# Tap weights broadcast over 128 rows of a cleared tile, six constant matmuls ahead of it, and a new order of all engines in a gated long convolution with a SwiGLU block

## The chip, the cores and the metric

The kernel runs on one core of one Trainium2 chip. The metric is the device time of one execution in microseconds (us); for several runs of one kernel the median is given. Beside the timed runs there is one profiled execution, whose span is the time from its first instruction to its last.

## The reference

Sequence length S = 2048, width D = 640, F = 1728, one batch, bfloat16. The input A_q is also the residual stream.

```python
x = A_q
h  = x + A(layernorm(x), A_k, A_v, A_shift_k, A_ssm_k, A_ssm_D)
h2 = h + B(layernorm(h), B_w_gate, B_w_up, B_w_down)

def A(q, k, v, shift_k, ssm_k, ssm_D):
    k_shift[s, d] = sum over t in 0..3 of k[s - 3 + t, d] * shift_k[d, 3 - t]   # causal, four taps
    kv = k_shift * v
    y  = causal convolution of kv with ssm_k along s (length 2048, by FFT), to bfloat16
    return q * (y + kv * ssm_D)

def B(x, w_gate, w_up, w_down):
    return (silu(x @ w_gate) * (x @ w_up)) @ w_down
```

The layer norms have no weights; eps is 1e-5.

## The kernel before

**Tiling.** The sequence is cut into four blocks of 512 tokens, the digit i in the names below. Tokens of a block lie on 128 partitions with four tokens to a partition (j = 0 to 3), so a block of q, k, v or of the output is a tile of 128 x 4 x 640. The long convolution is done per block in a transform domain, by matmuls with cosine and sine tables: forward transforms of the signal and of the filter, products of signal block j with filter block i - j that are summed for output block i, and an inverse transform.

**Steps and their names.** One function call builds a list of some 800 small tasks with names; each is one instruction, or for PE a short run of matmuls.

- "ident", "wrow", "k00", "k02", "kc0", "v0", "x0" and so on are loads (`load`, L446 to L449, the DMA is issued at L447). "k00" and "k02" bring token columns j = 0, 1 and j = 2, 3 of block 0 of k into k0n, "wrow" the four tap weights of each channel into two rows of the tile wrow. `tload` (L449, L450) is a load that transposes. "wrow", "drow" are issued on ACT's queue, the others on SP's.
- "zmem" (L497, POOL) fills a spare stretch of gu with ones. `filler` (L499 to L502) issues matmuls of 512 columns on it whose result nobody reads; PLAN's "fills" says ahead of which task and how many.
- "wb0", "wb4" (L510): the tap weights are spread over all partitions by matmuls of `halfrow` (two rows of ones, each for half of the partitions) with the two rows of wrow, 256 columns each, four matmuls and one. "diag0", "diag4" (L516, DVE) multiply the result with an identity, which gives the diagonal matrices of the taps.
- "k0tC.J" (L528): PE transposes block 0 of k, 20 matmuls against the identity in idall ("ident"), each for one token column J, five channel chunks C. "k0e0", "k0e2", "k0e4" copy the three results from PSUM to kT0 (L455 on ACT, L457 on DVE).
- "tpI.C" (L731): the taps as matmuls with the diagonals, in runs of 14 or 28 matmuls. "kvI.C" (L749 for block 0, L742 after) multiplies with v on DVE; for blocks 1 to 3 "keI.C" (L455) first copies PSUM into XT, which occupies the same memory as XH, the transform of the signal block two before.
- "ktM.P", "kteM.P" (L547, L455 or L457): the same transposing for filter block M. "kfM.", "xfI." are the forward transforms on PE (filter L581; signal L599 for block 0, L619 for the others), with "e" (L455, L458) for their copies from PSUM; "kb", "xb" are their additions on DVE.
- "pJI" (L777): the products on DVE, with letters a to d for their steps and "e" for the sum into the block's accumulator Y, on DVE or as an accumulating DMA. Such a DMA is `addto` (L567, L568): issued on POOL's queue, it adds one SBUF tile to another. "p02.e" adds the tile tt to Y, and p12.0a writes tt next.
- "ybI", "ivI.J" (L919, L924): the inverse transform. "ivI.Je, g, m, s, v, r, n": scaling on ACT (L934), gate by q on DVE (L941), mean and square sum on ACT (L840, L842), 1/sqrt on DVE and POOL (L835, L837), normalising on DVE (L981). "laI" are the same steps of the first layer norm.
- "htI.J" (L883): an SP-issued transposing DMA that writes the normalised 128 tokens into hnT. "fgI.HG", "fuI.HG" (L1029): gate and up matmuls of half H (256 tokens; half 0 needs htI.0 and htI.1, half 1 needs htI.2 and htI.3), group G, 20 matmuls or fewer. "sg", "su", "sv" (L1037, L1042, L1046, L1048) are their evacuations on ACT, "mu" (L1050) the product on DVE, "gd" a small copy.
- "dnI.J" (L1115, L992): the down projection, 28 matmuls. "rsI.J" writes it plus the mean to RB (L1131 on ACT, L1132 on DVE), "raI.J" is an accumulating DMA that adds RB to the residual in xh, and "outI.J" (L1144, SP) stores it. RB is one buffer. For block 3 the sum is done on DVE (L1136, L998). "xI" (L479) loads q of block I into the same xh that block I - 2 used.

**The order.** PLAN (L256 to L305) lists for each engine (pe, act, dve, pool, sp) the task numbers in the order in which the engine runs them, and for every PSUM tile which of four units of two banks it takes ("units"). An engine never runs a later task first. `add` (L92) finds what each task depends on from the memory that it reads and writes; `arrange` (L134) applies the plan, and makes the first writer of a PSUM tile wait for the readers of the tile that had the unit before; `emit` (L180) puts out the waits. A wait blocks all that stands behind it on that engine or queue.

```python
ident, id64, halfrow = idall[:, 0:P], idall[:, P:P + 64], idall[0:2, P + 64:P + 64 + P]   # L421
load("wrow", wrow[0:2], A_shift_k.rearrange("(c r x) k -> r c x k", r=2, x=64), 20000, "act")   # L469
last = e.matmul(pt.f(b // 2, 256, o=256 * (b % 2)), halfrow, wrow[0:2, c0 + b].rearrange("p x u -> p u x"), start=True, stop=True)   # L510
```

Of the kernel before, what the change touches and what calls it, by code (L numbers as in the profile page):

```python
# [12 lines left out]
P = 128  # L13
# [37 lines left out]
class _Graph:  # L51
# [128 lines left out]
    def emit(self, block):  # L180
# [74 lines left out]

PLAN = {  # L256
# [9 lines left out]
    "act":  # L266
# [10 lines left out]
    "dve":  # L277
# [10 lines left out]
    "pool":  # L288
        "19 17 15 16 125 165 174 158 192 183 223 225 224 342 396 362 281 371 285 401 380 289 406 389 343 293 420 415 527 466 "
        "470 561 474 552 478 579 570 684 586 591 529 705 710 698 637 732 723 641 645 750 649 741 "  # L290
        "",
    "sp":
        "0 2 3 8 4 6 10 7 230 9 11 13 14 235 296 226 12 229 297 227 481 231 167 176 228 234 295 233 194 185 482 232 364 282 373 "
        "290 391 294 286 382 480 653 652 471 563 554 467 475 479 581 572 651 734 725 638 752 646 743 642 650 798 807 801 804 "
        "810 "
        "",
    "units":
        "0131203132312001201201213230032110213023012230313133033220021021122013200230230222110332013110130232003210332301202110"
        "01310112312301210312031012210230131023033303012010313012013"
        "",  # L300
    "fills": {
        "wb0": ["zmem", 3],
        "k0t4.0": ["zmem", 1],
    },
}  # L305

# [1 line left out]
def bass_sequential_preLN__ssm_conv_h3__swiglu_ffn__prompt_kernel(  # L308
# [70 lines left out]
    with ExitStack() as es:  # L379
# [4 lines left out]
        def sb(name, off, shape, dty=bf):  # L384
            size = int(np.prod(shape)) * (4 if dty == f32 else 2)
            top[0] = max(top[0], off + size)
            return nc.alloc_sbuf_tensor_at(name, [P] + list(shape), dty, offset=A0 + off, align_bytes=32)
# [30 lines left out]
        kvo = sb("kvo", 179616, [4, D])  # L418
        diag = sb("diag", 184736, [NC5, 4, 64])
        idall = sb("idall", 187296, [P + 64 + P])  # L420
        ident, id64, halfrow = idall[:, 0:P], idall[:, P:P + 64], idall[0:2, P + 64:P + 64 + P]  # L421
        OS = sb("OS", 189856, [2, 2, D])
        RB = sb("RB", 187936, [D])
        bns = sb("bns", 187936 + 1280, [4, 2, 6], f32)
# [5 lines left out]
        o = 210336  # L430
# [9 lines left out]
        wrow = sb("wrow", 99840, [NC5, 64, 4])  # L440
# [3 lines left out]
        g = _Graph(nc, es)  # L444

        def load(name, dst, src, kb, engs="sp", **kw):  # L446
            return g.add(name, engs, lambda e, n: e.dma_start(dst, src), ("ld", kb), w=[dst], dma=True, **kw)  # L447
# [18 lines left out]
            load("kc%d" % m, kc[m][:], A_ssm_k[:, N * m:N * (m + 1)].rearrange("(c p) s -> p c s", p=P), 655360)  # L466

        load("ident", idall[:], id_d.ap(), 81920)
        load("wrow", wrow[0:2], A_shift_k.rearrange("(c r x) k -> r c x k", r=2, x=64), 20000, "act")  # L469
        for j in (0, 2):  # L470
            load("k0%d" % j, k0n[:, j:j + 2, :], tokens(K2, 0)[:, j:j + 2, :], 327680)
# [33 lines left out]
        for c0, nc_ in ((0, 4), (4, 1)):  # L505
            pt = g.tile()

            def mm(e, n, pt=pt, c0=c0, nc_=nc_):
                for b in range(nc_):
                    last = e.matmul(pt.f(b // 2, 256, o=256 * (b % 2)), halfrow, wrow[0:2, c0 + b].rearrange("p x u -> p u x"), start=True, stop=True)  # L510
                return last

            g.add("wb%d" % c0, "pe", mm, ("mm", 256, nc_), r=[halfrow, wrow[0:2]], pw=[pt])
            d = diag[:, c0:c0 + nc_].rearrange("p c u x -> p (c u) x")
            ib = id64.unsqueeze(1).to_broadcast([P, 4 * nc_, 64])
            g.add("diag%d" % c0, "dve", lambda e, n, pt=pt, d=d, ib=ib, nc_=nc_: e.tensor_tensor(  # L516
                out=d, in0=ib, in1=pt.f(0, 256 * nc_).rearrange("p (a x) -> p a x", x=64), op=ALU.mult),
                  ("ps", 256 * nc_), r=[id64], w=[d], pr=[pt])
# [52 lines left out]
        def halves(name, src, ev, od, scale, rot):  # L571
            for f in range(2):
                for par in (1, 0):
                    for cs in range(2):
                        pt = g.tile()
                        js = (par, par + 2)

                        def mm(e, n, pt=pt, f=f, cs=cs, js=js):
                            for j in js:
                                for c in range(2):  # L580
                                    last = e.matmul(pt.f(c, W), tab[:, f, cs, j], src[:, j, c * W:(c + 1) * W],  # L581
                                                    start=(j == js[0]), stop=(j == js[1]))
                            return last

                        g.add("%s.%d%d%d" % (name, f, par, cs), "pe", mm, ("mm", W, 4), r=[tab[:, f, cs]] + [src[:, j, :] for j in js], pw=[pt])
                        pl, sg = turn(cs, rot)
                        d = (od if par else ev)[:, f, pl, :]
                        evac("%se.%d%d%d" % (name, f, par, cs), (d, d.rearrange("p (b x) -> p b x", b=2)), lambda pt=pt: pt.f2(W), D, pt, sg * scale)
# [637 lines left out]
```

## Time and profile before

| what | value |
|---|---|
| timed runs | 260.73, 259.1, 261.67 us; median 260.73 |
| the profiled execution | 259.3 us, span 257.3 us |
| PE, DVE, ACT, POOL busy | 249.3, 200.0, 184.5, 58.5 us |
| first transpose (L528) | 4.66 us after the start of the span |
| first matmul of the signal's transform (L599) | 12.24 us |
| accumulating DMAs of 640 KB, issue to landing | C<-US 5.9 (median of 6), C<-K3r 7.9, Y<-US 6.5, Y<-tt 8.4 us |
| accumulating DMAs of 160 KB (xh<-RB) | 3.0 us, median of 12 |

Engines: PE does matmuls and PEld its weight loads, which overlap; DVE, ACT and POOL are the vector, scalar and general engines; SP issues DMAs. A line of the timeline has start, duration, engine, line of the kernel, operation, output<-inputs, count, and in brackets the idle time before it with what ended it. A busy PE is a modelled span, and single matmuls overlap, so counts times mean exceed the busy time. The chain that ended last is followed back from the last instruction to what released each step. The names there are those of the tiles, not of the tasks.

### The profile page before, as it was taken

How to read it: one execution, taken by the hardware profiler on the slowest of the kernel's cores; microseconds unless marked ns; L12 is line 12 of the kernel's file. 1: busy time of each engine (PE TensorE's matmuls, PEld its weight loads, DVE VectorE, ACT ScalarE, POOL GpSimd, SP SyncE). 2: the span in 40 equal slices, each digit the busy share in tenths (PEclk: the TensorE clock that was granted, in tenths of full speed). 3: DMA queues.
4: the chain of work that ended last, by engine and by line, in shares of the span. 5: the costliest groups of instructions: out<-in, count | busy, mean ns of one | idle time of the engine just before them, and what ended most of it. 6: DMA issues, size and time to landing. Idle time of an engine off the chain costs nothing.

```text
span 257.3 us, 5303 instructions
## 1 busy us (share of the span) xinstructions
PE 249.3 (97%) x2253; PEld 195.1 (76%) x2253; DVE 200.0 (78%) x256; ACT 184.5 (72%) x302; POOL 58.5 (23%) x56
## 2 busy tenths in 40 slices
PE   7999997999999999979999999999999999999995
PEld 4878773587888766868888866788886678888763
DVE  3689999999999998999999988999958524211242
ACT  2489999999996894577899789749981854516410
POOL 1001003082312052860030813333230314000000
PEclk9999999999999999999999999999999999999999
DMA  6998946788994058786946035497870152700011
GB/s 220 335 328 210 402 155 133 221 205 190 329 190 87 0 82 124 128 164 153 273 87 124 3 51 117 118 221 133 148 135 3 25 104 33 149 0 3 0 42 60
DMA packets 37620, 35.29 MB, mean 137 GB/s; under 512 B 21203, under 2 KB 32478, under 8 KB 37598
## 3 DMA queue, kind: packets, MB, share of 16 engines
q1 hardware_dynamic: 31792, 23.82, 33.2%
q0 software_dynamic: 5792, 11.14, 25.1%
q8 instruction: 17, 0.28, 0.5%
q14 instruction: 5, 0.04, 0.1%
q10 hardware_dynamic: 14, 0.01, 0.0%
HBM read 16.55 MB, written 2.62 MB: 75 GB/s over the span
## 4 chain that ended last, share of the span: by engine, by line
PE 62%; DVE 20%; ACT 11%; DMA 5%; issue 1%; SPq 0%; DVEq 0%
PE ps L1029 32%; PE ps L1115 16%; DVE tt L777 6%; PE ps L599 3%; DMA Y<-tt 3%; DVE Y L777 3%; PE ps L731 2%; ACT KO L455 2%; PE ps L919 2%; ACT C L455 2%; PE ps L581 2%; DVE C L777 2%; PE ps L992 2%; PE ps L619 2%; DMA k0n<-in_A_k_dram 1%; DVE gu L1050 1%
## 5 line engine op out<-in xcount | busy, mean ns | idle before, releaser
L1115 PE MATMUL ps<-Wd,gu 128*128 128x320 bf16 (+1 forms) x420 | 58.7, 300 | 0.0
L1115 PEld LDWEIGHTS ps<-Wd,gu 128*128 128x128 bf16 (+1 forms) x420 | 38.7, 97 | 18.4 <-issue 3.6
L777 DVE TENSOR_TENSOR tt<-XH,C 128x2560 bf16<-128x2560 bf16 (+1 forms) x31 | 47.8, 1571 | 1.5 <-DMA Y<-tt 0.9
L1050 DVE TENSOR_TENSOR gu<-gu,ub 128x1024 bf16<-128x1024 bf16 (+1 forms) x32 | 19.8, 620 | 26.2 <-ACT gu L1037 13.7
L1037 ACT ACTIVATE gu<-ps 128x1024 bf16<-128x1024 f32 (+1 forms) x32 | 29.4, 923 | 12.1 <-PE ps L1029 12.0
L1029 PE MATMUL ps<-hnT,GB 128*128 128x256 bf16 x280 | 34.0, 273 | 0.9 <-ACT XT L455 0.9
L1042 ACT ACTIVATE ub<-ps 128x1024 bf16<-128x1024 f32 x24 | 24.6, 1024 | 13.3 <-PE ps L1029 11.5
L1029 PE MATMUL ps<-hnT,UB 128*128 128x256 bf16 x280 | 33.8, 273 | 0.0
L1029 PEld LDWEIGHTS ps<-hnT,GB 128*128 128x128 bf16 x280 | 27.3, 98 | 4.3 <-ACT XT L455 1.0
L1029 PEld LDWEIGHTS ps<-hnT,UB 128*128 128x128 bf16 x280 | 27.3, 98 | 3.4 <-ACT KO L455 0.2
L1029 PE MATMUL ps<-hnT,GA 128*128 128x256 bf16 x240 | 28.8, 273 | 0.0
L1029 PE MATMUL ps<-hnT,UA 128*128 128x256 bf16 x240 | 28.5, 273 | 0.1
L837 POOL TENSOR_TENSOR mv<-mv,half 128x1 f32<-128x1 f32 x16 | 21.3, 1335 | 24.7 <-DVE mv L835 24.7
L1029 PEld LDWEIGHTS ps<-hnT,UA 128*128 128x128 bf16 x240 | 23.4, 98 | 3.4 <-ACT C L455 0.5
L1029 PEld LDWEIGHTS ps<-hnT,GA 128*128 128x128 bf16 x240 | 23.4, 98 | 3.2 <-DVE XH L458 0.3
L840 ACT ACTIVATE qo<-xh 128x640 bf16<-128x640 bf16 x28 | 21.0, 749 | 5.7 <-DMA xh<-in_A_q_dram 3.2
L581 PE MATMUL ps<-KT,tab 128*128 128x320 bf16 x128 | 19.6, 300 | 1.6 <-ACT K3r L455 0.7
L934 ACT ACTIVATE qo<-ps,one,st 128x640 bf16<-128x640 f32 x16 | 13.7, 886 | 9.8 <-PE ps L919 9.0
L568 POOL DMA_DIRECT2D xh<-RB x12 | 10.7, 888 | 34.7 <-DVE RB L1132 23.2
L581 PEld LDWEIGHTS ps<-KT,tab 128*128 128x128 bf16 x128 | 11.5, 98 | 8.2 <-ACT K3r L455 1.6
L837 POOL TENSOR_TENSOR st<-st,half 128x4 f32<-128x4 f32 x4 | 7.9, 1986 | 33.6 <-DVE st L832 21.8
L455 ACT ACTIVATE XH<-ps 128x640 bf16<-128x640 f32 x19 | 13.3, 736 | 1.5 <-PE ps L619 0.7
(112 smaller groups left out, 384.8 us busy)
## 6 DMA issues: line engine op xcount, KB each, us to landing
C<-US POOLq DMA_DIRECT2D x6, 640.0 KB, 5.9
kc<-in_A_ssm_k_dram SPq DMA_DIRECT2D x4, 640.0 KB, 10.6
xh<-in_A_q_dram SPq DMA_DIRECT2D x4, 640.0 KB, 5.5
out_dram<-xh SPq DMA_DIRECT2D x15, 160.0 KB, 2.0
kvo<-in_A_v_dram SPq DMA_DIRECT2D x3, 640.0 KB, 4.4
xh<-RB POOLq DMA_DIRECT2D x12, 160.0 KB, 3.0
Wd<-in_B_w_down_dram SPq DMA_DIRECT2D x1, 1280.0 KB, 7.8
C<-K3r POOLq DMA_DIRECT2D x2, 640.0 KB, 7.9
```

Of the source, the lines that this page charges most:

```text
L455: return e.activation(out=dst[1], in_=src(), func=ACTF.Copy, scale=scale)
L568: return g.add(name, "pool", lambda e, n: e.dma_start(dst, src, accum_op=ALU.add, max_dma_last_dim=4096), ("acc", 2 * int(np.prod(dst.shap ...
L581: last = e.matmul(pt.f(c, W), tab[:, f, cs, j], src[:, j, c * W:(c + 1) * W], start=(j == js[0]), stop=(j == js[1]))
L777: g.add(nm, "dve", lambda e, n_: e.tensor_tensor(out=d, in0=a, in1=b, op=op), ("sb", n * D), r=[a, b], w=[d])
L837: g.add(name + "r", "pool", lambda e, n: e.tensor_tensor(out=dst, in0=tmp, in1=hf, op=ALU.pow), ("pp", 4), r=[tmp, half[:]], w=[dst])
L840: g.add(name + "m", "act", lambda e, n: e.activation(out=junk, in_=x, func=ACTF.Identity, scale=-1.0 / D, accum_out=sm), ("aa", D, 0), r=[ ...
L934: g.add(nm + "e", "act", lambda e, n, pt=pt, q2=q2, s=s, j=j: e.activation(out=q2, in_=pt.f2(W), func=ACTF.Identity, scale=s[:, 3, j:j + 1 ...
L1029: last = e.matmul(pt.f(q // 2, 256, o=256 * (q % 2)), w[:, c, f0:f0 + P], hnT[:, c, cols], start=(c == 0), stop=(c == NC5 - 1))
L1037: g.add("sg%d.%d%d" % (i, h, gp), "act", lambda e, n, pa=pa, gv=gv, nf=nf: e.activation(out=gv, in_=pa.f(0, 256 * nf).rearrange("p (f x) - ...
L1042: g.add("su%d.%d%d" % (i, h, gp), "act", lambda e, n, pb=pb: e.activation(out=ub[:].rearrange("p b x -> p (b x)"), in_=pb.f(0, 1024), func ...
L1050: g.add("mu%d.%d%d" % (i, h, gp), "dve", lambda e, n, gv=gv, ubv=ubv: e.tensor_tensor(out=gv, in0=gv, in1=ubv, op=ALU.mult), ("sb", 256 * ...
L1115: last = e.matmul(pt.f(c, W), gu[k, fb, col(i, j)], Wd[k, fb, c * W:(c + 1) * W], start=st, stop=sp)
```

## The change

One task is added, "wz": a memset of the whole tile wrow (128 x 1280 bfloat16) to zero on DVE, ahead of the load "wrow", which then writes its two rows. The broadcast reads all 128 rows of wrow and of halfrow, whose rows 2 to 127 are zeros in the constant that is loaded; the sums are the same. All task numbers but the first rise by one. PLAN's lists are new for every engine. The fillers are six ahead of "wb4", which now comes first, where there were three ahead of "wb0" and one ahead of "k0t4.0".

```diff
     "fills": {
-        "wb0": ["zmem", 3],
-        "k0t4.0": ["zmem", 1],
+        "wb4": ["zmem", 6],
     },
...
-        ident, id64, halfrow = idall[:, 0:P], idall[:, P:P + 64], idall[0:2, P + 64:P + 64 + P]
+        ident, id64, halfrow = idall[:, 0:P], idall[:, P:P + 64], idall[:, P + 64:P + 64 + P]
...
         load("ident", idall[:], id_d.ap(), 81920)
+        g.add("wz", "dve pool", lambda e, n: e.memset(wrow[:], 0.0), ("pm", 1280), w=[wrow[:]])
         load("wrow", wrow[0:2], A_shift_k.rearrange("(c r x) k -> r c x k", r=2, x=64), 20000, "act")
...
-                    last = e.matmul(pt.f(b // 2, 256, o=256 * (b % 2)), halfrow, wrow[0:2, c0 + b].rearrange("p x u -> p u x"), start=True, stop=True)
+                    last = e.matmul(pt.f(b // 2, 256, o=256 * (b % 2)), halfrow, wrow[:, c0 + b].rearrange("p x u -> p u x"), start=True, stop=True)
...
-            g.add("wb%d" % c0, "pe", mm, ("mm", 256, nc_), r=[halfrow, wrow[0:2]], pw=[pt])
+            g.add("wb%d" % c0, "pe", mm, ("mm", 256, nc_), r=[halfrow, wrow[:]], pw=[pt])
```

The same tasks run on the same engines but for these: to ACT from DVE k0e4, kte0.0, kf0e.011, xf3e.10, la3.0x, rs2.2; to DVE from ACT kf0e.110, la2.3x, xf3e.31, xf3e.21, la3.1x; lp0 to POOL and lp2 to DVE. The lists in names, where the order differs and the text below speaks of it ("-" before, "+" after):

```
sp, start
- ident k00 k02 v0 kc0 tab0 x0 tab1 PKg ntab kc1
+ k02 ident k00 v0 kc0 tab0 x0 tab1 ntab kc1 kc2
act, start
- wrow warm drow k0e2 k0e0 kte0.1 xf0e.01 xf0e.00
+ wrow warm drow k0e4 k0e2 k0e0 kte0.0 kte0.1 xf0e.01 xf0e.00
dve, start
- diag4 diag0 k0e4 kv0.4 kv0.2 kv0.3 kv0.1 kv0.0 kte0.0 drowadd
+ wz diag4 diag0 kv0.4 kv0.3 kv0.2 kv0.0 kv0.1 drowadd
pe, start
- wb0 wb4 k0t4.0 k0t4.1 k0t0.0 k0t2.0 k0t2.1 k0t4.2 k0t4.3 k0t2.2 k0t2.3 k0t0.1 k0t0.2 k0t0.3 tp0.4 tp0.2 tp0.0
+ wb4 wb0 k0t4.0 k0t2.0 k0t4.1 k0t4.2 k0t2.1 k0t4.3 k0t2.2 k0t2.3 k0t0.0 k0t0.1 k0t0.2 k0t0.3 tp0.4 tp0.2 tp0.0
pe, up to the first F0 tasks
- kf2.000 xf1.10 xf1.01 fu0.00 xf1.20 xf1.00 fg0.00 xf1.21 fg0.01
+ xf1.00 xf1.10 kf2.111 xf1.30 fg0.00 xf1.01 xf1.21 fu0.00 fg0.01
dve, around p02 and p12
- p02.c mu0.11 p02.b mu0.12 iv1.1g p12.0b mu0.13 iv1.0v iv1.3g p12.0d iv1.0n p12.1b iv1.1v iv1.2g p12.1d iv1.1n p12.0a
+ p02.c p02.b mu0.11 iv1.0v p12.0b mu0.12 iv1.1g p12.0d mu0.13 iv1.2g p12.1b iv1.1v iv1.0n p12.1d iv1.3g iv1.1n p12.0a
dve, after p12
- p12.0c p12.1a p12.1c iv1.2v p03.b iv1.3v p03.a iv1.2n p03.c mu1.00 kv2.2 kv2.0 kv2.4 p03.d
+ p12.0c p12.1a p12.1c iv1.3v p03.b iv1.2v p03.a iv1.3n p03.c mu1.00 kv2.4 p03.d kv2.0 kv2.2
pe, blocks 1 and 2
- dn0.1 dn0.2 dn0.3 fu1.00 fg1.00 tp2.2 tp2.0 tp2.4 fg1.02 xf2.30 xf2.31 fg1.01 xf2.10
+ dn0.1 iv1.3 dn0.3 dn0.2 fu1.00 fg1.00 tp2.0 tp2.4 tp2.2 fg1.02 fg1.01 xf2.20 xf2.30 fu1.01
act, there
- su1.00 sg1.00 ke2.2 ke2.0 ke2.4 rs0.3 sg1.02
+ su1.00 sg1.00 ke2.4 ke2.0 ke2.2 rs0.3 sg1.02
sp, there
- WdA ht1.0 out0.0 ht1.1 out0.2 ht1.3 out0.3 out0.1 ht1.2 x2
+ WdA ht1.0 v2 ht1.1 out0.1 out0.2 out0.3 out0.0 ht1.3 ht1.2 x2
```

More of the change, by code (lines that the diff above doesn't have):

```diff
@@ L257 @@
     "pe":
[7 rows of a table removed]
[7 rows of a table added]
         "",
     "act":
[9 rows of a table removed]
[9 rows of a table added]
         "",
     "dve":
[9 rows of a table removed]
[9 rows of a table added]
         "",
     "pool":
-        "19 17 15 16 125 165 174 158 192 183 223 225 224 342 396 362 281 371 285 401 380 289 406 389 343 293 420 415 527 466 "
-        "470 561 474 552 478 579 570 684 586 591 529 705 710 698 637 732 723 641 645 750 649 741 "
+        "20 17 16 18 126 166 175 159 193 184 224 226 127 225 343 397 363 282 372 344 286 402 390 290 407 381 294 421 416 467 "
+        "528 471 562 475 553 479 580 571 685 587 592 706 711 699 638 733 724 642 742 646 751 650 "
         "",
     "sp":
-        "0 2 3 8 4 6 10 7 230 9 11 13 14 235 296 226 12 229 297 227 481 231 167 176 228 234 295 233 194 185 482 232 364 282 373 "
-        "290 391 294 286 382 480 653 652 471 563 554 467 475 479 581 572 651 734 725 638 752 646 743 642 650 798 807 801 804 "
-        "810 "
+        "4 0 3 9 5 7 11 8 10 12 14 297 13 15 232 298 230 227 228 231 236 482 168 177 229 296 235 234 195 186 233 365 483 374 "
+        "287 291 295 283 392 383 481 653 654 564 555 476 472 468 480 582 573 652 735 726 753 744 647 802 651 639 643 799 805 "
+        "808 811 "
         "",
     "units":
-        "0131203132312001201201213230032110213023012230313133033220021021122013200230230222110332013110130232003210332301202110"
-        "01310112312301210312031012210230131023033303012010313012013"
+        "1003210213032103213231202021313201203032301220202331231313213020231003323102103013012121102232313302203202110131231102"
+        "10233202102301032132021013330301202312022200212003130123021"
         "",
     "fills": {
-        "wb0": ["zmem", 3],
-        "k0t4.0": ["zmem", 1],
+        "wb4": ["zmem", 6],
     },
```

50 rows, old and new, of the table PLAN are left out of this document.

## The prediction

> **What bounds the kernel now.** I read the page's busy times and the shares of the chain that ended last, then the chain in order of time, then busy time by stage, then single instructions where PE or DVE stood still.
>
> ```profile
> PE 249.3 (97%) x2253; PEld 195.1 (76%) x2253; DVE 200.0 (78%) x256; ACT 184.5 (72%) x302; POOL 58.5 (23%) x56
> ...
> PE 62%; DVE 20%; ACT 11%; DMA 5%; issue 1%; SPq 0%; DVEq 0%
> ```
>
> PE is busy 249.3 of 257.3 us, so an order alone can win back at most the 8.0 us that are left, less what lies before the first load and after the last matmul. Busy time by stage (PE, PEld, DVE, ACT, POOL) says where:
>
> ```profile
> 40.00:50.00 10.00, 7.93 (x49) 3.55 (x48) 9.62 (x12) 10.00 (x19) 2.38 (x2) 1.00 0.68 152
> 50.00:92.00 42.00, 42.00 (x368) 34.91 (x367) 41.97 (x43) 38.50 (x67) 12.36 (x8) 1.00 0.67 168
> ...
> 109.00:115.00 6.00, 4.63 (x80) 3.90 (x75) 6.00 (x8) 4.49 (x7) 4.28 (x4) 1.00 0.87 164
> 115.00:160.00 45.00, 45.00 (x425) 35.98 (x423) 43.18 (x56) 38.79 (x68) 10.71 (x8) 1.00 0.53 114
> ```
>
> From 40 to 50 ACT is full and PE loses 2.07 us. From 50 to 92 PE and DVE are both full. From 109 to 115 PE loses 1.37 us while DVE is full. After that PE is full to the end but for 0.25 us near 160. The chain shows the start, and the one long transfer on it (start us, us, what):
>
> ```profile
> 1.14 3.47 DMA k0n<-in_A_k_dram
> ...
> 4.66 2.31 PE ps L528 x20
> 6.97 2.70 PE ps L731 x42
> ...
> 9.70 1.76 DVE kvo L749 x3
> ...
> 12.24 2.35 PE ps L599 x16
> ...
> 91.64 8.39 DMA Y<-tt
> ```
>
> The timeline shows the matmuls of the start, and the two waits that the transfer leads to:
>
> ```profile
> 1.30 1.46 PE L502 MATMUL ps<-gu 128*128 128x512 bf16 x3 [1.30 <-POOL gu L497]
> ...
> 2.76 1.29 PE L510 MATMUL ps<-wrow,idall 2*128 2x256 bf16 x5
> ...
> 4.66 2.31 PE L528 MATMUL ps<-idall,k0n 128*128 128x128 bf16 x20
> ...
> 10.63 1.31 PE L547 MATMUL ps<-idall,kc 128*128 128x128 bf16 x20
> ```
> ```profile
> 100.05 1.49 DVE L777 TENSOR_TENSOR tt<-XH,C 128x2560 bf16<-128x2560 bf16 x1 [0.90 <-DMA Y<-tt]
> ...
> 111.63 2.36 PE L1029 MATMUL ps<-hnT,GB 128*128 128x256 bf16 x20 [0.88 <-ACT XT L455]
> ```
>
> Twenty transposes take 2.31 us at 4.66 and 1.31 at 10.63: PE runs at half its rate for about the first ten microseconds, though the page's clock row reads 9 throughout. The activity before that was 1.46 us of fillers, 1.29 us of matmuls on two rows, one more filler (0.61), transposes, and taps (L731) from 6.9.
>
> The profiled run took 259.3 us, 2.0 around its span. The three timed runs are 259.1, 260.73 and 261.67, so it lies 1.4 under the median. I sum against 259.3.
>
> **The clearing and the tap load.** "wz" is new and first on DVE, which now idles until 4.09, so on DVE it costs nothing. But ACT's "wrow" load must now wait for it. No row shows a DVE memset. POOL's take 0.52 us for 512 elements and 0.16 for 80, 0.83 ns an element, so 1280 would take 1.2. Two of DVE's 128x640 tensor_scalars (0.38 each) make 0.8. I take 1.2, nearest in operation; nothing below zero, as an instruction is added. It runs from 0.7 to 1.9. The load was issued at 0.73 and its matmul ran at 2.73, so it lands 2.0 after issue, at 3.9 (3.5 to 4.0). Queued behind it on ACT are "warm" and "drow", not needed before 6.3. [...]
>
> **Six fillers and the taps' broadcast.** Fillers start 0.43 us apart in the trace: six occupy 1.30 to 3.9, against three and one before. The tap load lands then too, so each covers the other. The five broadcast matmuls took 1.29 us on two rows; on 128 rows a filler streams 512 columns in 0.43, so 256 take 0.22, and I keep 1.2 for five (1.1 to 1.3). PE is free at 5.1, was 4.66. That is hidden: "k02", "ident", "k00" replaces "ident", "k00", "k02" on SP, three loads of unchanged total. The two k0n loads land after 3.47 and, from the median of 3.6 for both, about 3.75: at 4.6 and 5.4. Whichever is last lands at 5.4, and now it holds the token columns that PE transposes first. So the twenty transposes start at 5.45, not 4.66.
>
> From there the price hangs on PE's rate. At half rate everything to the first L599 matmul moves by the same 0.8: 12.24 becomes 13.0. At full rate: eight transposes and their drain, 0.75; three PSUM copies, now all on ACT (0.55, 0.95, 0.95), the second done at +2.25; 28 taps, 0.91 plus drain 0.2 (70 take 2.28 later in the chain), +3.4; four products on DVE at 0.62, +5.9. That is 11.4, a gain of 0.8. If the rate rises only after the transposes it is 11.9 to 12.2. I take 11.7 between them, a gain of 0.5. Moving "kte0.0" (1.24) to ACT falls into ACT's 3.67 us of idle time before 11.98 and frees 0.81 of DVE ahead of "p00", which waits for ACT anyway (23.7). I count both at nothing; without the cover, 0.6.
>
> Will the rate rise? With the change PE has 128-row matmuls from 1.3 to 5.1, 3.8 us with no gap but a few tenths. In the trace the taps, 6.9 to 10.7, are the only stretch as long without a transpose, and the rate rises in it or at its end. I say yes.
>
> **The order from 57 on.** DVE's waits set p12.0a: the transfer p02.e (Y<-tt) is issued when p02.b ends. Before, 13 DVE steps stand between p02.b and p12.0a; now mu0.11 (0.6) is moved behind p02.b, making 14. So p02.b ends 0.6 earlier, at 90.7; the transfer of 8.4 from 91.0 ends at 99.4; the 14 steps, 7.9 us, end at 98.6. p12.0a goes from 100.05 to 99.4: 0.65 gained. From p12.0a to p03.a the steps are the same 10.5 us, and "ke2.4" to "ke2.2" wait for p03.a because XT lies over XH: 110.5 becomes 109.9. fg1.02 needs "ke2.4" now, the short copy, first on ACT: PE's 1.0 us wait goes, and two F1 tasks stand ahead of the first xf2, so its 0.5 goes too. What is late next is iv2.1: yb2.4 ends at 149.7 today, with PE there at 149.8. The DVE steps between p03.a and yb2.4 are the same set in both orders (39.2 us), so PE waits there for all it won beyond 0.65. That is the term: −0.65. Ends: 0 (the transfer slower by as much as it starts earlier) and −1.4 (DVE also saves its 0.46 and 0.9 of waits).
>
> **The rest.** Up to the first F0 task ACT does the same copies and statistics: 28.3 plus 23.1 us of rows ends "xf1e.30" at 51.4, against "xf1e.01" at 51.1 with one copy more left to do. No change, ±0.4. From 160 on, la2.3x, xf3e.31 and .21 come to DVE and la3.0x, rs2.2 go to ACT. DVE is 52% busy from 165 to 254, so nothing; the pieces up to dn3.3c are the same PE work.
>
> Sum: 259.3 − 0.5 − 0.65 = 258.15, said as 258.2.
>
> **Rivals.** *The rate rises no earlier (0.22).* Then the 0.5 is lost and 0.8 paid: 259.45 if it rises where it did, and up to the 2.4 by which the slowest run exceeds the profiled one if it rises later: 259.5 to 261.9. For it: the same kernel's runs spread over 2.6 us, which a rate that rises at different moments would give. The fillers before also ran 1.4 us on 128 rows without raising it. [...]
>
> *SP's queue blocks the next transposes (0.21), slower than before.* "ht1.3" and "ht1.2" (L883) now stand behind "out0.3" and "out0.0", which wait for the accumulating transfer of RB. By rows, rs0.3 ends at 113.1, ra0.3 issues at 113.2, lands 3.2 later, and ht1.2 lands at 121.3; PE wants it at 123.3. It decides once that transfer takes over 5.2 us. The longest such today is 4.8, but Y<-tt took 8.4 and one C<-US 9.8: 3 to 5 us of PE wait, and x2 (L479) behind it delays the next layer norm as much. 260.5 to 265.
>
> *The new order closes more of the ACT-bound gap (0.13).* The 2.07 us at 40 to 50 and 1.4 at 109 to 115 could both go if DVE follows: 255.6 to 257.2. Against it: the ACT sum above.
>
> **The numbers.** Forecast 258.2, chance 0.44, own range 257.2 to 259.6. What a measurement of this kernel can tell is about 1%, so the limits are 258.1 and 263.3. Faster: 0.20 of the forecast and all of the third rival, 0.33. Slower: half of the queue's case and a little of the clock's, 0.13. Within: 0.54. The range leaves out the lower part of the third rival and the upper of the queue's: 256.3 to 262.6.
>
> **What would show it.** Twenty L528 transposes in about 1.2 us; the first L599 matmul at 11.4 to 12.0; "wrow" landing near 3.9; p12.0a 0.65 earlier, counted from p02.b's stage; no PE wait before L1029 near 111, one before L919 near 149. Wrong would be: transposes of 0.11 us each, L599 at 13 or later; an idle PE before an L1029 near 123; an ACT-bound gap well off 2 us.

## The result, and the profile after

| kernel | median of its runs | ratio |
|---|---|---|
| before | 260.91 us (259.1 to 261.67, six runs) | |
| after | 264.41 us (262.83 to 265.56, six runs) | 1.0139 (95% interval 1.0095 to 1.0184) |

The change makes the kernel slower. The profiled execution after took 264.23 us with a span of 262.3, against 259.3 and 257.3. On other chips the kernel before took 258.1 to 258.7 us, so every experiment below is compared with the kernel before as it was timed beside it on the same chip. Medians are over all runs of a kernel, while the ratios leave out single runs that lie over 1.5% above the fastest of their kernel, so a ratio can differ from that of the two medians.

The first view is the page's busy times and its chain of waits by engine:

```profile
PE 249.9 (95%) x2255; PEld 194.6 (74%) x2255; DVE 200.1 (76%) x256; ACT 186.1 (71%) x303; POOL 73.1 (28%) x56
...
PE 59%; DVE 25%; POOL 10%; DMA 3%; ACT 2%; issue 1%; SPq 0%; DVEq 0%; ACTq 0%
...
L837 POOL TENSOR_TENSOR st<-st,half 128x4 f32<-128x4 f32 x4 | 22.6, 5641 | 30.7 <-DVE st L832 24.8
```

All engines are as busy as before but one: POOL has 73.1 us in place of 58.5, and 10% of the chain, where it had no share that was shown. Four instructions account for it, the 1/sqrt of the first layer norm (L837, "laIr", 128x4). They average 5641 ns; the same row of the kernel before has 7.9 us in all and 1986 ns:

```profile
L837 POOL TENSOR_TENSOR st<-st,half 128x4 f32<-128x4 f32 x4 | 7.9, 1986 | 33.6 <-DVE st L832 21.8
```

By stage after the change (columns as before):

```profile
40.00:50.00 10.00, 7.57 (x47) 3.53 (x45) 9.56 (x12) 10.00 (x20) 2.86 (x2) 1.00 0.61 125
50.00:92.00 42.00, 38.89 (x337) 32.51 (x338) 38.88 (x38) 35.74 (x61) 23.02 (x8) 0.98 0.65 158
...
90.30:93.60 3.30, 3.30 (x14) 1.86 (x13) 2.88 (x3) 2.74 (x6) 0.00 (x0) 0.50 0.00 0
109.00:115.00 6.00, 6.00 (x86) 5.28 (x86) 6.00 (x5) 2.84 (x3) 5.09 (x4) 1.00 0.83 157
115.00:160.00 45.00, 44.23 (x448) 36.16 (x443) 43.12 (x54) 37.97 (x62) 14.90 (x7) 1.00 0.55 114
```

PE's wait at 109 to 115 is gone, as predicted. But from 50 to 92, where PE had been full, it now stands for 3.1 us, and after that it runs at a granted clock of 0.50 for a while. The chain, in order of time, names the wait, the timeline of PE shows its length, and the timeline of DVE shows what ran beside it:

```profile
78.81 10.09 POOL st L837
...
88.99 0.89 ACT qo L934
...
89.93 2.06 PE ps L924 x8
```
```profile
89.93 2.06 PE L924 MATMUL ps<-Y,itab 128*128 128x320 bf16 x8 [3.11 <-ACT qo L934]
```
```profile
78.56 0.17 DVE L835 TENSOR_SCALAR st<-st 128x4 f32<-128x4 f32 x1
78.63 1.49 DVE L777 TENSOR_TENSOR Y<-Y,tt 128x2560 bf16<-128x2560 bf16 x1
80.03 0.42 DVE L1050 TENSOR_TENSOR gu<-gu,ub 128x512 bf16<-128x512 bf16 x1
...
85.17 2.82 DVE L777 TENSOR_TENSOR Y<-XH,C 128x5120 bf16<-128x5120 bf16 x1
90.68 0.49 DVE L941 TENSOR_TENSOR xh<-xh,qo 128x640 bf16<-128x640 bf16 x1 [2.69 <-ACT qo L934]
```

la1v (the 128x4 step at 78.56) releases la1r on POOL. La1r then takes 10.08 us. In the kernel before it took 1.40:

```profile
77.76 1.40 POOL L837 TENSOR_TENSOR st<-st,half 128x4 f32<-128x4 f32 x1 [1.72 <-DVE st L835]
```

After the change DVE runs seven two-input steps without a gap to 87.99, and la1r ends at 88.89, 0.90 after them. ACT's iv1.1e needs its result, PE needs the PSUM unit that iv1.1e frees: PE has no matmul from 86.82 to 89.93. After that idle time the clock is granted at 0.50 for 3.41 us, in which PE runs at half its rate (an L1115 matmul every 0.27 us in place of 0.14). Starts of single tasks, with "+" for later than before: iv1.0 −1.66 (it comes earlier in the order), dn0.1 +3.98, iv2.1 +3.60, dn1.2 +4.53, the last matmuls +4.99. The step from iv2.1 to dn1.2 is the same thing once more: la2r took 9.17 us (4.42 before), DVE's la2w had to wait for it, and the copy behind la2w on DVE (L1092) kept PE waiting for 0.77 us:

```profile
145.71 9.17 POOL L837 TENSOR_TENSOR st<-st,half 128x4 f32<-128x4 f32 x1 [0.31 <-DVE st L835]
```
```profile
155.39 1.80 PE L1115 MATMUL ps<-Wd,gu 128*128 128x320 bf16 x12 [0.77 <-DVE gu L1092]
```

The start, first PE's timeline, then the chain:

```profile
1.30 2.74 PE L502 MATMUL ps<-gu 128*128 128x512 bf16 x6 [1.30 <-POOL half L490]
3.94 1.30 PE L510 MATMUL ps<-wrow,idall 128*128 128x256 bf16 x5
6.15 1.29 PE L528 MATMUL ps<-idall,k0n 128*128 128x128 bf16 x20 [0.91 <-DMA k0n<-in_A_k_dram]
```
```profile
2.12 6.82 DMA v<-in_A_v_dram
...
9.04 1.44 DVE kvo L749 x3
...
12.17 2.35 PE ps L599 x16
```

The twenty transposes take 1.29 us in place of 2.31: in this execution PE's rate did rise early. But they begin at 6.15, and then the load of v0 ends last, at 8.94, so the first L599 matmul is at 12.17 against 12.24.

### The profile page after: what moved, and what is told of

It reads as the page before. It is cut to its first block, busy times and chain, and to the rows that moved or that the text cites. A ratio compares the mean times of both kernels' runs of the same rounds, so it can differ in the third digit from the quotient of the medians.

```text
span 262.3 us, 5303 instructions
## 1 busy us (share of the span) xinstructions
PE 249.9 (95%) x2255; PEld 194.6 (74%) x2255; DVE 200.1 (76%) x256; ACT 186.1 (71%) x303; POOL 73.1 (28%) x56
## 4 chain that ended last, share of the span: by engine, by line
PE 59%; DVE 25%; POOL 10%; DMA 3%; ACT 2%; issue 1%; SPq 0%; DVEq 0%; ACTq 0%
PE ps L1029 28%; PE ps L1115 19%; DVE tt L777 8%; POOL st L837 7%; PE ps L599 3%; DVE Y L777 3%; DVE XH L634 3%; DMA v<-in_A_v_dram 3%; POOL mv L837 2%; PE ps L581 2%; DVE C L561 2%; PE ps L992 2%; PE ps L919 1%; PE ps L924 1%; DVE gu L1050 1%
## 5 line engine op out<-in xcount | busy, mean ns | idle before, releaser
L1115 PE MATMUL ps<-Wd,gu 128*128 128x320 bf16 (+1 forms) x420 | 59.7, 302 | 0.8 <-DVE gu L1092 0.8
L1115 PEld LDWEIGHTS ps<-Wd,gu 128*128 128x128 bf16 (+1 forms) x420 | 39.2, 99 | 20.2 <-issue 3.9
L1029 PE MATMUL ps<-hnT,UB 128*128 128x256 bf16 x280 | 33.9, 273 | 0.0
L1029 PE MATMUL ps<-hnT,GB 128*128 128x256 bf16 x280 | 33.5, 273 | 0.0
L837 POOL TENSOR_TENSOR st<-st,half 128x4 f32<-128x4 f32 x4 | 22.6, 5641 | 30.7 <-DVE st L832 24.8
L1029 PEld LDWEIGHTS ps<-hnT,UB 128*128 128x128 bf16 x280 | 27.3, 98 | 3.5 <-ACT ub L1042 0.3
L1029 PEld LDWEIGHTS ps<-hnT,GB 128*128 128x128 bf16 x280 | 27.1, 98 | 3.5 <-ACT KO L454 0.2
L1029 PE MATMUL ps<-hnT,GA 128*128 128x256 bf16 x240 | 28.7, 273 | 0.1
L1029 PE MATMUL ps<-hnT,UA 128*128 128x256 bf16 x240 | 28.2, 273 | 0.2 <-issue 0.2
L837 POOL TENSOR_TENSOR mv<-mv,half 128x1 f32<-128x1 f32 x16 | 19.5, 1219 | 29.5 <-DVE mv L835 29.5
L1029 PEld LDWEIGHTS ps<-hnT,GA 128*128 128x128 bf16 x240 | 23.4, 98 | 3.4 <-ACT OS L454 0.5
L1029 PEld LDWEIGHTS ps<-hnT,UA 128*128 128x128 bf16 x240 | 23.3, 98 | 3.4 <-issue 0.5
L568 POOL DMA_DIRECT2D C<-US x6 | 7.2, 1288 | 26.7 <-DVE US L777 26.7
```

What stands on the lines that cost most here:

```text
L568: return g.add(name, "pool", lambda e, n: e.dma_start(dst, src, accum_op=ALU.add, max_dma_last_dim=4096), ("acc", 2 * int(np.prod(dst.shap ...
L837: g.add(name + "r", "pool", lambda e, n: e.tensor_tensor(out=dst, in0=tmp, in1=hf, op=ALU.pow), ("pp", 4), r=[tmp, half[:]], w=[dst])
L1029: last = e.matmul(pt.f(q // 2, 256, o=256 * (q % 2)), w[:, c, f0:f0 + P], hnT[:, c, cols], start=(c == 0), stop=(c == NC5 - 1))
L1115: last = e.matmul(pt.f(c, W), gu[k, fb, col(i, j)], Wd[k, fb, c * W:(c + 1) * W], start=st, stop=sp)
```

## The experiments

Theory P: POOL's 128x4 steps are held by DVE's train of two-input steps, because the new order puts la1v behind mu0.02 and la2v behind p22.1d. Theory R: the order on PE or the new start is slower in itself. Theory Q: POOL's own queue. The first four runs shared one chip (kernel before 258.07 us); the changed kernel itself was not timed on it.

**la1v put back.** The changed kernel, in DVE's list:

```diff
- p11.1c mu0.02 la1v p11.1e
+ p11.1c la1v mu0.02 p11.1e
```

> The changed kernel with one DVE step moved by one place: la1v (the step that lets POOL's la1r begin) stands ahead of mu0.02 again, as in the kernel before. Theory P (la1r, a POOL operation that reads SBUF, cannot begin while DVE runs two-input operations without a gap; ACT's iv1 scaling waits for it, PE stands still for 3.3 us and then runs 3.4 us at half its clock): if one earlier place lets la1r slip in as before, la1r takes 1 to 2 us instead of 10.1, no PE wait at 86.5, no 0.50 clock, and the time falls by 3.5 to 4.5 us to 260 to 261; if it does not slip in, la1r takes 10 to 11 us and nothing changes. Theory Q (POOL's own queue, with lp0 and the issue of kc3.0 ahead, holds la1r): la1r still ends near 88.9, time unchanged. Theory R (the order of PE and the start cost the time, la1r only happens to be late): time stays above 263 even where la1r is short.

261.17 us, ratio 1.0130 (1.0097 to 1.0164). POOL's timeline of this kernel:

```profile
79.20 1.41 POOL L836 TENSOR_TENSOR st<-st,half 128x4 f32<-128x4 f32 x1 [2.86 <-DVE st L834]
```

One place in DVE's list takes la1r from 10.08 to 1.41 us. PE has no wait at 86, the clock stays at 1.00, and dn0.1 comes at +0.01 where it was +3.98. La2r remains at 9.16, with a gap of 1.25 us between two PE starts behind it. The timed ratio alone would not show the gain, as it is hardly under the 1.0139 of the change on its chip; the comparison on one chip follows below ("Both steps moved").

**DVE made to yield.** The changed kernel, with p11.1e waiting for la1r:

```diff
+        for name, other in (("p11.1e", "la1r"), ):
+            byname[name].deps.add(byname[other])
```

> The changed kernel with one dependency added: DVE's p11.1e, which follows la1v, waits for la1r to end. Nothing else is changed. Theory P: DVE stands idle for about 1.0 us, la1r takes 0.9 to 1.2 us instead of 10.1, the PE wait at 86.5 and the halved clock go; PE's loss of 3.3 + 1.7 us becomes at most the 1 us that DVE loses: 260.5 to 261.5. Theory Q: la1r takes 10 us all the same, DVE waits for all of it, and the time rises to 270 or more. Theory R: la1r short, the time stays above 263.

262.08 us, 1.0173 (1.0137 to 1.0208). La1r took 1.04 us, the shortest in any of the whole kernels, so it is DVE that held it and not POOL's queue:

```profile
79.90 1.04 POOL L838 TENSOR_TENSOR st<-st,half 128x4 f32<-128x4 f32 x1 [3.29 <-DVE st L836]
```
The 1.17 us that DVE gives up come back as PE gaps of 1.11 at 83 and 0.44 at 86.

**Fillers over the wait.** The changed kernel with 14 fillers ahead of fu0.12:

```diff
+        "fu0.12": ["tab0", 14],
```

> The changed kernel with 14 matmuls of 512 columns whose result nobody reads ahead of fu0.12, so that PE is busy while it would stand still for iv1.1e. The wait itself stays: la1r still ends near 89. If the halved clock from 90.2 to 93.6 comes from the 3.4 us of standing still, it goes, and 14 matmuls in 3.3 us become some 25: 1.7 us less, 262.5 to 263. If the clock halves for another reason (or not because of this wait), it stays at 0.50 for 3.4 us and the time is unchanged or up to 0.3 us longer.

262.92 us, 1.0210 (1.0171 to 1.0249). La1r still takes 10.08 and iv1.2 starts at 89.88, but the granted clock stays at 1.00 (the 1.00 behind the busy times), and dn0.1 starts at 94.75 in place of 96.47:

```profile
90.00:94.00 4.00, 4.00 (x31) 2.87 (x30) 3.33 (x4) 3.01 (x6) 0.00 (x0) 1.00 0.00 0
```

So the half clock is worth 1.7 us at that point and follows from the idle time. Of these, 1.0 to 1.2 us are left at the last matmuls, counted from the first L599 matmul against the two executions of the change.

**The fault alone.** The kernel before with la1v behind mu0.02:

> The kernel before with one DVE step moved by one place: la1v behind mu0.02, as in the changed kernel. Theory P: la1r now begins inside p11.1e and is held until DVE has a gap; that is 8 to 10 us, iv1.1e and iv1.0e are late, PE stands still near 86 for about 2 to 3.4 us; time 263 to 265.5. If the boundaries between DVE steps let la1r in by chance, it may be 1 to 5 us long and the time stays 260 to 261.5. Theories Q and R: no change, 260.9.

261.03 us, 1.0122 (1.0065 to 1.0179): +3.0 us from one exchange of two DVE steps. La1r took 10.08, PE's starts were 3.03 us apart at 86, and the clock was 0.50 for 3.41:

```profile
78.05 10.08 POOL L836 TENSOR_TENSOR st<-st,half 128x4 f32<-128x4 f32 x1 [2.45 <-DVE st L834]
```

**Both steps moved.** On a second chip (kernel before 258.65) the changed kernel was run again beside a version with la1v put back and, around la2v, the order of before (yb2.1 la2v p22.1c p22.1d):

> The changed kernel once more, beside the kernel before on the chip that the next three are timed on, as their base. If la1r's 10.1 us follow from the order of DVE's steps, they come again to 0.1 us, with PE's wait near 86.5 and 3.4 us at half the clock; 264 to 265.

> The changed kernel with la1v ahead of mu0.02 (which made la1r 1.4 us in the first such run) and, in addition, the five DVE steps around la2v in the order of the kernel before (yb2.1, la2v, p22.1c, p22.1d). Theory P: la2r is held by DVE too; 9.2 us becomes 4.4 or so if the boundary that let it in before is still one, PE's wait of 1.1 us ahead of dn1.1 goes and the time is 0.5 to 1.1 us under the 261.2 that la1v alone gave. If la2r stays at 9 us: the boundary (before yb2.2, which the changed order gives to mu1.11) decides, and the time stays at 261.2.

The change again: 265.05 us, 1.0181 (1.0104 to 1.0258). The version: 260.44, 1.0055 (1.0016 to 1.0094). On one chip, then, most of the loss goes with la1v's place. But la2r still took 9.16 us there, so its place after yb2.1 was not what had let it in.

**The start alone.** On the same chip, the kernel before with wz, the 128-row broadcast and its six fillers, and the kernel before with SP's loads in the order k02 ident k00:

> The kernel before, with the cleared tile, the broadcast over 128 rows and six fillers ahead of wb0, none ahead of k0t4.0; every order as before. It tells the start's own part apart from the order. If full-rate matmuls come earlier because of it, the first L599 matmul comes 0.3 to 0.8 us earlier than in the kernel before and the time falls by as much; if PE is only occupied longer ahead of the first transposes (5.2 instead of 4.5 to 4.7), 0.3 to 0.8 us are lost. The late part stays: la1r 1.4 us, no wait at 86.5.

> The kernel before with SP's first three loads in the changed order alone: k02, ident, k00 instead of ident, k00, k02. The transposes of token columns 0 and 1 go first on PE in both. If the last of the loads now holds them, the first transpose moves from 4.5 to about 6.2 and the first L599 matmul later by 0.8 to 1.5, and so the time; if the transposes that follow were waiting for the last load anyway, less than 0.4.

259.01 us, 0.9994 (0.9955 to 1.0033), and 259.19 us, 0.9999 (0.9962 to 1.0035). Full clock came at 5.83 with the broadcast (9.82 in the kernel before) and the first L599 at 12.29; with the load order alone they came at 10.70 and 13.22. The moment of full clock is not the same from one execution to the next: it was 4.89 in the profiled execution of the change and 9.32 in its repetition. Of all twelve profiled executions of whole kernels with the new broadcast, eight had the twenty transposes in 1.29 to 2.11 us and the first L599 matmul at 11.7 to 12.3; in the other four, the repetition among them, the transposes took 2.3 and L599 came at 12.9 to 13.3. So an early rise of the rate goes with an L599 about 1 us earlier, but the new start does not make sure of it, and it begins the transposes later (5.0 to 6.3 us, with the whole old start 4.4 to 4.7). The mean of L599 is the same: 12.3 for the twelve, and 12.3 for the five executions without the broadcast (11.0 to 13.2).

**POOL's step beside plain streams.** A kernel of its own, nothing of the reference computed: one pow beside twelve DVE steps at a time.

> Nothing of the reference is computed here: only POOL's pow of 128x4 (twice 128x1) f32, fifteen times, each released after the first (once the second) instruction of a fresh stream of twelve DVE instructions. Theory P (a POOL step that meets a running train of two-input DVE instructions is held until the train has a gap, its length does not depend on the pow): alone 1.0 to 1.1 us; beside twelve additions of 128x1280 bfloat16 (0.82 each, eleven left) 9 to 10 us, one less of 0.82 when released after the second; beside one-input copies 1.1 to 2; beside twelve of 128x640 about 5.3 and of 128x2560 about 17; with a tiny one-input step as the fifth of the stream, or a DVE wait for the pow ahead of the fifth, about 3.4. Where each DVE step waits for its predecessor there is a gap of 0.03 us at every boundary, and the pow gets in at the first: 1.9. Where each waits for a semaphore that was reached long before there is no gap: 9 to 10. Theory Q (POOL merely runs slower beside any DVE work, by a factor): all streams alike, the one-input copies as well, and no dependence on the number of instructions left.

Theory P as I had it falls. Alone the 128x4 pow took 1.02 us; beside additions of 128x1280 1.52, of 128x2560 2.19, of 128x640 1.19, beside copies 1.20. Each ended about 0.9 us after the first boundary between two DVE steps, whatever was still to come, also where the second of two steps without a gap released it. A train that has no gap does not hold POOL as such.

**Both mended, and mu0.11 alone.** The version with both steps moved, and in it p22.1e followed by yb2.2, which waits for it; and the kernel before with mu0.11 behind p02.b, which was the prediction's gain. The lists show DVE's order in the changed kernel and in the first of the two, behind la2v:

```diff
- yb2.0 p22.1e mu1.11 yb2.3 yb2.2
+ yb2.0 mu1.11 p22.1e yb2.2 yb2.3
```

> The changed kernel with la1v ahead of mu0.02, and around la2v the DVE order yb2.1 la2v p22.1c p22.1d yb2.0 mu1.11 p22.1e yb2.2 yb2.3, so that p22.1e is followed by the step that waits for it. Theory P (all of the loss is the two held POOL steps, which end where DVE has a gap): la1r 1.4 us, la2r 4 to 5.2 us in place of 9.2, PE's wait of 1.07 us ahead of the block-2 down projection gone, dn1.2 at +0.0 to +0.2 against the kernel before, and the ratio 1.000 to 1.003. Theory R (the order itself is slower): la2r short but the ratio stays at 1.004 to 1.007. If yb2.2 gives no gap: la2r 9.2 and the ratio 1.0055 as with la1v alone mended.

> The kernel before with one DVE step moved: mu0.11 behind p02.b. The prediction's step: p02.b and its transfer 0.6 us earlier, p12.0a 0.65 earlier, PE's later waits shorter by as much, ratio 0.9975 (258.0 against 258.65). Rival: PE waits for mu0.11 or for something else that is as late, p12.0a earlier but dn1.2 and the end within 0.1 of before, ratio 0.999 to 1.001. Rival that loses: mu0.11 holds up su0.12 and the F0 tasks by 0.9, ratio above 1.002.

Kernel before 258.31. The first: 259.52 us, 1.0049 (1.0024 to 1.0073). POOL's timeline:

```profile
77.83 1.40 POOL L836 TENSOR_TENSOR st<-st,half 128x4 f32<-128x4 f32 x1 [2.77 <-DVE st L834]
...
141.58 5.02 POOL L836 TENSOR_TENSOR st<-st,half 128x4 f32<-128x4 f32 x1 [0.71 <-DVE st L834]
```

La2r is down from 9.16 to 5.02, and both PE waits are gone: dn1.2 stands 138.66 us after the first L599 (before 138.62), the last matmuls 240.27 (240.21). La2r now ends 0.9 us after the wait of yb2.2, a gap of 0.035 us on DVE; in the kernel before its 4.42 us end in the same way, and with 9.17 it ends 0.9 us after the first gap too. Against this one profile of the kernel before nothing of the loss is left, and nothing is won either. But that profile has the latest iv2.1 of the old order, 137.53 after the first L599. The three profiled executions that change the start alone have it at 136.98 to 137.16, the two of the mended version with la1r in time at 137.55 and 137.56. The difference of 0.4 to 0.6 arises on DVE: the same steps from the end of p03.a to the end of yb2.4 take 39.56 us in the mended version and 39.19 in the kernel before.

The second: 258.88 us, 1.0023 (0.9998 to 1.0049). Counted from the first L599, p02.b came 0.48 earlier and p12.0a 0.32 later, because of a new wait in DVE's timeline:

```profile
92.66 0.69 DVE L1049 TENSOR_TENSOR gu<-gu,ub 128x1024 bf16<-128x1024 bf16 x1 [1.09 <-ACT ub L1041]
```

Mu0.11 frees the one buffer ub. Later by 1.5 us, it lets ACT's su0.12 start later, and mu0.12 behind it waits 1.09.

**The kernel's own DVE steps, alone, then with company.** Two kernels that run la1v, la1r and the train of p11.1e to p02.a on cleared tiles, and compute nothing of the reference. The first has nothing else:

> Nothing of the reference is computed: DVE runs la1v and then its own steps of the kernel on cleared tiles, POOL runs la1r (released by la1v), and PE, ACT and the DMA queues stand still. Three trains first: p11.1e mu0.03 yb1.0 mu0.10 yb1.1 p02.d p02.a (9.5 us of DVE, the order after), the same with mu0.02 ahead (the order before), the first again. Then pairs of neighbours from the two orders, one for each boundary. Theory P (DVE's steps alone hold POOL): la1r takes 10 us beside the first and third train and 1.4 beside the second, as in the two kernels, and the pairs show which boundary lets it in (it ends 0.9 us after the first step of the pair) and which doesn't (0.9 after the second). Theory S (something else of the kernel has a part: ACT, PE, a transfer, POOL's earlier work): no la1r over 2.6 us in any train, each ends 0.9 us after the first boundary.

La1r took 2.11, 1.32 and 2.11 us in the three trains, and ended 0.9 after the first boundary there and in every pair. Something else had a part. The second adds one thing at a time, three times over:

> Nothing of the reference is computed. The same DVE train with la1v and POOL's la1r as in the run of DVE's steps alone (2.1 us there), three times over, now: alone; with five two-input steps running ahead of la1v, in the order after (mu0.02 la1v) and before (la1v mu0.02); with each DVE step waiting for an event long past; beside ACT copies from SBUF, ACT copies from PSUM, PE matmuls, loads from HBM, an accumulating DMA from POOL's queue; and all together in both orders. Theory T (a DVE that has been running holds on): 10 us with steps ahead, 2.1 without. Theory C (company): 10 us beside the one that matters, and beside all together. Theory E (a race of a few ns that the kernel's timing mostly loses): some of the three repeats 10 us and others 2.1, in no fixed place. If all are 2.1 or less, none of these is the cause, and it stays open.

POOL's timeline, for the first three stretches (alone; five steps ahead and the order after; five steps ahead and the order before), and for the last two (all company, the order after, the order before):

```profile
37.17 2.09 POOL L808 TENSOR_TENSOR st<-st,half 128x4 f32<-128x4 f32 x1 [1.42 <-DVE st L806]
53.05 9.97 POOL L808 TENSOR_TENSOR st<-st,half 128x4 f32<-128x4 f32 x1 [13.79 <-DVE st L806]
69.25 1.29 POOL L808 TENSOR_TENSOR st<-st,half 128x4 f32<-128x4 f32 x1 [6.23 <-DVE st L806]
...
162.80 10.08 POOL L808 TENSOR_TENSOR st<-st,half 128x4 f32<-128x4 f32 x1 [8.00 <-DVE st L806]
...
181.21 1.39 POOL L808 TENSOR_TENSOR st<-st,half 128x4 f32<-128x4 f32 x1 [6.57 <-DVE st L806]
```

With DVE idle before la1v, la1r took 2.09 or less in every round, beside ACT, PE, loads or an accumulating DMA alike; 0.03 us of idle time, in which la1v waits for the step ahead of it, were enough. With five two-input steps running ahead without a gap and la1v last before the train, 9.97 in three rounds of three, and 10.08 with company in three of three, exactly the kernel's number. With mu0.02 between, 1.29 to 1.39 in five rounds of six, and once 10.57. So it is a DVE that runs into la1v without a gap that holds POOL over the boundaries, the other engines have no part, and the order decides, almost always. The profiled executions of the whole kernels agree: with la1v last before the train (and DVE not made to wait) 10.08 in four of four, with mu0.02 between 1.40 or 1.41 in eleven of twelve.

**Start or order.** On a fourth chip (kernel before 258.44): both steps mended with the old start; the same with the new start; the new start with the old order.

> The changed kernel with both held steps mended, and the start put back: two-row broadcast without the clearing, fillers three and one, SP's loads ident k00 k02. If the start is what is still slower: ratio 0.998 to 1.002, and less than e14's by 0.003 to 0.005. If the order is: 1.004 to 1.006, as e14.

> The changed kernel with both held steps mended, again, beside e13 and e15 on one chip. 1.003 to 1.006 by the run before of the same kernel; profile as there: la1r 1.40, la2r 5.02, PE from the first L599 to the end as long as before to 0.1 us.

> The kernel before with the change's start alone (clearing, 128-row broadcast, six fillers), again. If the start is what is still slower: 1.003 to 1.005. If the order is: 0.998 to 1.001, as in the run before of the same kernel (0.9994, interval 0.9955 to 1.0033).

260.13 us, 1.0046 (1.0019 to 1.0073); 260.02, 1.0062 (1.0041 to 1.0083); 258.63, 1.0008 (0.9984 to 1.0032). The start costs and gains nothing on the median; the order costs about 0.5% even with both steps mended. In the profiled execution of the first, la1r took 10.68 us although la1v stood ahead of mu0.02: the rare miss, in a whole kernel.

```profile
78.70 10.68 POOL L836 TENSOR_TENSOR st<-st,half 128x4 f32<-128x4 f32 x1 [2.60 <-DVE st L834]
```

That execution took 264.21 us, with a mean granted clock of 0.993, which is what 3.41 us at half clock make of the whole. A mean of 0.994 or less stands beside 8 of the 10 timed runs of the change, and beside 6 of the 90 of the kernel before on the five chips of the experiments (261.3 to 263.0 us). So the old order too seems to stall PE this long now and then; that la1r is the cause in these runs is not shown.

**Where the order costs it.** The new order up to 90 and up to 150 us, the old one behind:

> The changed kernel with both held steps mended up to 90 us (ahead of p02.b on DVE, iv1.3 on PE), the old order from there. If the new order costs its 0.5% before 90: ratio 1.003 to 1.006. If after: 0.998 to 1.002.

> The same with the new order up to 150 us (ahead of gd1.1 on DVE, dn1.2 on PE) and the old one from there. If the cost is after 150: 0.998 to 1.002; if between 90 and 150: 1.003 to 1.006 here and 1.000 with the new order up to 90 alone.

265.15 us, 1.0264 (1.0210 to 1.0318), and 262.09, 1.0148 (1.0091 to 1.0205). Both seams made waits of their own (4.5 us of PE for the buffer RB at 96 in the first, 1.5 at 152 for iv2.0e in the second), so these two tell nothing of the 0.5%.

## Why the prediction was wrong

It said 258.2 us, and slower with a chance of 0.13; the kernel became slower by 1.4%. Of the 6.2 us between the forecast and 264.41, 1.6 are its base: it summed against the profiled 259.3, not the median, which is 260.91 over six runs. The rest is a gain of 1.15 forecast and a loss of 3.5 measured.

- **The step that failed** is "The order from 57 on". It summed DVE's steps and followed ACT and PE, and took the POOL steps at the lengths they had. La1v moved behind mu0.02 was not costed at all, and neither was the new place of la2v. The runs show for the first +3.0 us alone in the kernel before, and for the second 0.9 to 1.1 us: dn1.2 starts 2.03 to 2.21 us after iv2.1 where la2r takes 9.2, and 1.10 before. The row that could have warned was there, though the prediction does not show it: the page of before has 1986 ns as the mean of four equal 128x4 steps, of which la1r took 1.40 and la2r 4.42, so the length of such a step was not a constant.
- **−0.65 from mu0.11** was not there. P02.b did come earlier, but the sum counted only whose turn comes sooner, and not that mu0.11 also frees ub: alone the move put p12.0a 0.32 us later. In the mended version, where p12.0b stands between, p12.0a came 0.33 earlier after the first L599 than in the profile of before (87.49 against 87.82), and that was gone by iv2.1 (137.56, before 137.53). The base was luck as well: the transfer of Y<-tt that the sum puts at 8.4 us took 6.7 to 8.0 in the three other profiles with the old order, and p12.0a stands at 87.28 to 87.45 in them, no later than in the mended version. And "the same set" of DVE steps up to yb2.4, 39.2 us, took 39.64 in the new order.
- **−0.5 from the start**: the rate rose early in the profiled execution (1.29 us for the transposes, full clock at 4.89), and the size was wrong: 0.07. The transposes began 0.7 later than I had them, on the k0n load, and then v0 ended last, a load that the sum did not follow. That the rate rose early was partly luck: it did so in eight of twelve executions with this start, and not in the repetition of the same kernel.
- **The tap load** as a term did not matter: wb4 waited for the load ident, which was issued at 1.19 and landed 2.7 later, and not for wrow, whose landing no row shows; so nothing measures the 3.5 to 4.0 given for it. The clearing took 0.59 us against 1.2, as it is issued as 640 elements and the sum counted 1280.
- **No PE wait near 111**: right, in the change (6.00 of 6.00 us) and in the mended version, where PE also has the wait that was forecast ahead of L919 near 149 (0.41 us).
- **The rivals.** The clock's did not come in the profiled execution, but in the repetition it did (full clock at 9.32, L599 at 12.86); it is worth about 1 us, not the loss. The queue's did not come: no wait ahead of the L1029 near 123 over 0.5 us. (The longest transfer of RB in the kernel before was 5.1 us, not 4.8; it lies late, at 206.) The third, closing the ACT-bound gap at 40 to 50, fell: PE loses 2.43 us there, before 2.07. The loss was none of them.

What stays open: 1.2 to 1.7 us between the mended versions and the kernel before in the timed runs, of which the profiled ones show 0.4 to 0.6 at iv2.1; and by what DVE's running train gets past a boundary at which a fresh one lets POOL in, while the bare streams, released by a two-input step, never held it.

## What to carry to other kernels

Before an order of DVE steps is changed, look for each small POOL step that a DVE step releases, and for what DVE runs right after it: let a gap (a step that waits for its predecessor) come soon after the release (the 0.035 us ahead of yb2.2 were enough for la2r), and price the POOL step at the whole train up to the next gap if there is none (10.08 us for la1r). In the bare runs a gap just ahead of the release did as well (la1r 2.12 us or less). One further step between the release and the train was enough for la1r nearly always (1.40 or 1.41 us in eleven of twelve whole kernels); la2r was held over four and five further steps, up to the gap (4.42 and 5.02 us). When a step is moved, follow the buffer that it frees as well as the one that it fills. An idle PE of 3 us cost 1.7 us more in granted clock; fillers took that part back, but not the wait.

## What the runs showed of the hardware

- A 128x4 pow on POOL took 1.02 us alone, and up to 10.7 us beside a DVE that was already running two-input steps without a gap; then it ended 0.9 us after the first gap. La1r took 1.04 us where DVE yielded and 10.08 where it did not, and the 10.08 spanned seven DVE instructions and the boundaries between them.
- The half clock lasted 3.41 us each time (in the change, its repetition, the kernel before with la1v late, the first seam, and the mended version with the held la1r), after gaps of 3.0 us or more between two PE starts; gaps up to 1.8 us in an execution at full clock brought none.
- Clearing 128x1280 bfloat16 on DVE is issued as 640 32-bit elements and took 0.59 us; in the run of the kernel's steps alone 1280 such elements took 1.12 us and 2560 took 2.19.
